# GpSimd copies released by the VectorE operation ahead of the planned SBUF copy instead of by the copy itself

## Chip, cores and metric

One core of one Trainium2 chip. The metric is the time of one execution in microseconds of device time, the median of several runs. The profiler's span of the same execution is about 1.8 us shorter than that time; trace times below count from the span's start.

## The reference, cut to what matters

```python
def reference(A_x, A_wqkv, A_wo, B_x, B_w_gate, B_w_up, B_w_down, gate_w):
    # x: 1 x 2048 x 512, bf16; 32 heads of 16; gated MLP of width 1376
    g = sigmoid((A_x * gate_w).sum(-1, keepdims=True))
    a = attention(A_x, A_wqkv, A_wo)      # softmax(q k^T / 4) v, then wo
    b = ((A_x @ B_w_gate) * (A_x @ B_w_up)) @ B_w_down
    return g * a + (1 - g) * b
```

The bulk is 32 heads x 2048 x 2048 exponentials of attention scores.

## The kernel before: the parts that the change touches

The exponentials are shared out. ScalarE computes most of them (line 1689: exp from PSUM into bf16 tiles in SBUF, 1024 or 1536 columns at a time). For the rest, VectorE evicts a score tile from PSUM (reads it there and writes it to SBUF) as an integer approximation of its exponential (line 1076), and the three other quarters of that key block are had from the same tile by adding a constant to the int16 pattern: an SBUF-to-SBUF copy, run either by VectorE (line 1154) or by GpSimd (line 1157):

```python
if eng == "dve":      # VectorE
    fn = lambda v: v.tensor_single_scalar(cell_ap(c, I16), cell_ap(src, I16), 32.0 * k, ALU.add)
else:                 # GpSimd
    fn = lambda g: g.tensor_scalar(cell_ap(c, I16), cell_ap(src, I16), 32.0 * k, 1.0, ALU.add, ALU.mult)
```

The kernel is laid out by a planner in Python, which keeps a clock per engine with assumed durations and appends each operation with its dependencies; semaphore waits are made from these. VectorE's copies and GpSimd's use the same pair of SBUF ports, called the port below, and the one that comes second waits (1.27 us for 0.41 in the lines at 73 us that the prediction shows). The planner keeps VectorE's copies and GpSimd's operations apart in time, and makes GpSimd wait on the chip for the last VectorE copy planned before it:

```python
def gen_step(eng):
    t = clock[eng]
    if eng == "pool" and t < lock["dve"]:          # GpSimd not during a VectorE copy
        clock[eng] = lock["dve"]
        return True
    ...                                            # best = a ready operation of the queue
    if eng in ("dve", "pool") and (best is None or best.prio > CPR):
        if eng == "pool" or lock["pool"] <= t:     # VectorE copy not during GpSimd
            c = try_copy(eng, t)
            if c is not None:
                if eng == "dve":
                    lock["op"] = c                 # the copy to wait for
                elif lock["op"] is not None:
                    c.deps.append(lock["op"])      # GpSimd waits for it
                run_task(c, t)
                lock[eng] = clock[eng]
                return True
    ...
    if eng == "pool" and lock["op"] is not None:
        best.deps.append(lock["op"])               # so do GpSimd's other operations
    run_task(best, t)
```

VectorE never waits for GpSimd for the port's sake; if GpSimd runs late, the two meet on the chip.

The softmax here doesn't subtract the row's maximum and nothing guards it: scores larger than these inputs give would overflow.

## Time and profile before

| | before |
|---|---|
| time, median (range, runs) | 715.96 us (715.78 to 716.11, 3) |
| span of the profiled run | 714.4 us, granted clock 0.998 |
| busy: TensorE, VectorE, ScalarE, GpSimd | 96%, 91%, 98%, 59% |
| longest chain | ScalarE 63%, GpSimd 0% |

The page's own lines are shown in the prediction.

### The profile page before, as it was taken

What the parts mean: (1) busy time and instruction counts of PE and PEld (TensorE: products, weight loads), DVE (VectorE), ACT (ScalarE), POOL (GpSimd) and SP (SyncE); (2) the same over time, 40 slices, a digit from 0 to 9 for tenths busy, and PEclk for the clock granted to TensorE, in tenths of its full rate; (3) what the DMA queues carried; (4) which work ended last, traced back from release to release, by engine and by line L of the source; (5) the groups of instructions that cost most, each with busy time, mean ns of one, the idle gap of its engine ahead of it and who ended that gap; (6) DMA issues with size and microseconds to landing.
All of it is one profiled execution on the core that took longest, in us unless ns stands there. A gap on an engine that the chain in (4) does not pass through costs nothing.

```text
span 714.4 us, 21301 instructions
## 1 busy us (share of the span) xinstructions
PE 687.7 (96%) x9115; PEld 188.3 (26%) x9115; DVE 649.1 (91%) x1229; ACT 699.9 (98%) x689; POOL 424.7 (59%) x463
## 2 busy tenths in 40 slices
PE   8999899999999999999999999999999999999997
PEld 3323232222222222222222222222222222222222
DVE  5999989998998889899988998999889988998887
ACT  6999999999999999999999999999999999999995
POOL 4547676555556575566477556555557676555572
PEclk9999999999999999999999999999999999999999
DMA  6800001000200001000000010000000001000001
GB/s 140 257 12 8 21 17 18 21 17 16 86 21 18 17 11 35 28 17 17 20 3 28 17 43 26 18 11 12 21 18 17 15 29 31 17 21 18 3 20 46
DMA packets 33054, 21.65 MB, mean 30 GB/s; under 512 B 20380, under 2 KB 27964, under 8 KB 32960
## 3 DMA queue, kind: packets, MB, share of 16 engines
q1 hardware_dynamic: 31632, 19.64, 9.4%
q8 instruction: 71, 1.16, 0.7%
q10 hardware_dynamic: 1328, 0.66, 0.4%
q14 instruction: 23, 0.19, 0.1%
HBM read 15.12 MB, written 2.36 MB: 24 GB/s over the span
## 4 chain that ended last, share of the span: by engine, by line
ACT 63%; PE 22%; DVE 8%; issue 3%; SPq 2%; DMA 1%; POOL 0%; DVEq 0%; POOLq 0%
ACT PT L1689 57%; PE psS L488 8%; PE psO L1219 7%; PE psX L557 5%; ACT wv L1689 4%; SPq L322 2%; ACT wd L1689 2%; DVE PT L1076 2%; DVE PT L1154 1%; DVE wd L1076 1%; PE psS L557 1%; PE psX L667 1%; DVE QM L632 1%; PE psX L488 1%; DMA xT<-in_A_x_dram 1%
## 5 line engine op out<-in xcount | busy, mean ns | idle before, releaser
L1689 ACT ACTIVATE PT<-psS 128x1024 bf16<-128x1024 f32 (+1 forms) x577 | 624.8, 1413 | 1.2 <-PE psS L488 0.8
L1157 POOL TENSOR_SCALAR PT<-PT 128x1024 int16<-128x1024 int16 x220 | 228.2, 1047 | 161.5 <-DVE PT L1154 81.2
L488 PE MATMUL psS<-QM,KE 32*128 32x512 bf16 x1968 | 255.4, 376 | 10.7 <-ACT PT L1689 5.4
L1076 DVE TENSOR_SCALAR PT<-psS 128x512 int16<-128x512 f32 x328 | 221.6, 684 | 22.5 <-PE psS L488 18.5
L1219 PE MATMUL psO<-PT,VS 128*18 128x512 bf16 x1709 | 227.9, 381 | 0.7 <-DVE oraw L1248 0.6
L1219 PE MATMUL psO<-PT,VD 128*18 128x512 bf16 x1231 | 192.3, 381 | 0.6 <-DVE wd L1154 0.6
L1017 PEld LDWEIGHTS <-KE 32*128 32x128 bf16 x2048 | 63.1, 91 | 278.1 <-issue 144.9
L1154 DVE TENSOR_SCALAR PT<-PT 128x1024 int16<-128x1024 int16 (+1 forms) x232 | 105.3, 482 | 2.2 <-PE psO L1219 1.0
L1157 POOL TENSOR_SCALAR PT<-wv 128x1024 int16<-128x1024 int16 x57 | 59.1, 1047 | 39.7 <-DVE PT L1154 15.0
L1219 PEld LDWEIGHTS psO<-PT,VS 128*18 128x18 bf16 x1709 | 52.1, 88 | 61.0 <-issue 43.6
L1689 ACT ACTIVATE wv<-psS 128x1024 bf16<-128x1024 f32 (+1 forms) x47 | 59.7, 1300 | 0.0
L557 PE MATMUL psX<-wd,hT 128*32 128x512 bf16 (+1 forms) x704 | 59.0, 386 | 0.0
L1076 DVE TENSOR_SCALAR wv<-psS 128x512 int16<-128x512 f32 x76 | 51.8, 686 | 6.2 <-PE psS L488 5.8
L1219 PEld LDWEIGHTS psO<-PT,VD 128*18 128x18 bf16 x1231 | 45.4, 88 | 36.9 <-issue 23.4
L557 PE MATMUL psX<-xT,wu 128*32 128x512 bf16 x688 | 53.2, 383 | 1.2 <-DVE wv L1076 0.8
L557 PE MATMUL psX<-xT,wg 128*32 128x512 bf16 x688 | 52.5, 383 | 1.5 <-DVE PT L1076 1.2
L1219 PE MATMUL psO<-wv,VS 128*18 128x512 bf16 x182 | 49.9, 381 | 0.2 <-DVE oraw L1248 0.2
L1076 DVE TENSOR_SCALAR PT<-psX 128x512 int16<-128x512 f32 x58 | 39.7, 684 | 6.8 <-PE psS L488 6.6
L1689 ACT ACTIVATE wd<-psS 128x1024 bf16<-128x1024 f32 (+1 forms) x35 | 40.3, 1222 | 0.4 <-PE psS L488 0.4
L1219 PE MATMUL psO<-wv,VD 128*18 128x512 bf16 x167 | 38.2, 381 | 0.0
L1157 POOL TENSOR_SCALAR wv<-PT 128x1024 int16<-128x1024 int16 x24 | 25.1, 1047 | 18.7 <-PE psO L1219 3.6
L488 PE MATMUL psX<-QM,KE 32*128 32x512 bf16 x80 | 30.1, 377 | 4.0 <-DVE VS L687 0.9
(127 smaller groups left out, 703.3 us busy)
## 6 DMA issues: line engine op xcount, KB each, us to landing
rb<-rscr SPq DMA_DIRECT2D x31, 256.0 KB
out_dram<-ost SPq DMA_DIRECT2D x12, 128.0 KB, 1.7
wu<-in_B_w_up_dram SPq DMA_DIRECT2D x1, 1376.0 KB, 9.2
wg<-in_B_w_gate_dram SPq DMA_DIRECT2D x1, 1376.0 KB, 12.1
wd<-in_B_w_down_dram SPq DMA_DIRECT2D x1, 1280.0 KB, 6.0
OT<-OX SPq DMA_DIRECT2D x60, 16.0 KB, 1.8
wo<-in_A_wo_dram SPq DMA_DIRECT2D x1, 512.0 KB, 12.6
out_dram<-wk SPq DMA_DIRECT2D x4, 128.0 KB, 1.7
```

Of the source, the lines that this page charges most:

```text
L322: return now(eng, deps, lambda e: e.dma_start(dst, src, **kw), occ, lat=lat, stream=stream, dma=True)
L488: return e.add_instruction(mybir.InstMatmult(name=nc.get_next_instruction_name(), engine=mybir.EngineType.PE, ins=[e.lower_ap(rhs), e.lowe ...
L557: return e.matmul(out_ap[32 * q : 32 * q + w, :], lhs[:, 32 * q : 32 * q + w], rhs, start=s0, stop=s1, tile_position=(0, 32 * q), skip_gro ...
L632: lambda v, p=p: v.tensor_scalar(QM[:, p, b, :], qtmp[:], mask[:, p : p + 1], None, ALU.mult),
L667: r = e.matmul(bk.ap[32 * q : 32 * q + 32, t2 * 256 : (t2 + 1) * 256], xT[:, kt, t * 128 + 32 * q : t * 128 + 32 * q + 32], wv[:, kt, bp * ...
L1017: r = e.ldweights(w, tile_position=pos)
L1076: lambda v: v.tensor_scalar(cell_ap(pr["cell"][i : i + 1], mybir.dt.int16), bk.ap, CB, 0.0, ALU.add, ALU.max),
L1154: fn = lambda v: v.tensor_single_scalar(cell_ap(c, I16), cell_ap(src, I16), 32.0 * k, ALU.add)
L1157: fn = lambda g: g.tensor_scalar(cell_ap(c, I16), cell_ap(src, I16), 32.0 * k, 1.0, ALU.add, ALU.mult)
L1219: r = e.matmul(psO[32 * j : 32 * j + VW, :], pv_stationary(m, kt, j, k), cell_ap((cell,)), start=s0, stop=s1, tile_position=(0, 32 * j), s ...
L1689: lambda a: a.activation(cell_ap(c), src, ACT.Exp, scale=LN2 / 128.0),
```

## The change

Intent: GpSimd should not lose the time of a semaphore's way after each VectorE copy. It is let go when the operation ahead of the copy ends; the copy, which follows at once, is expected to be on the shared port first and to hold GpSimd back by itself. Below, such a release of GpSimd around one VectorE copy is called a handover. The diff in its core:

```diff
-        lock = {"dve": 0.0, "pool": 0.0, "op": None}
+        lock = {"dve": 0.0, "pool": 0.0, "op": None, "prev": None}
...
                         if eng == "dve":
-                            lock["op"] = c
+                            lock["op"] = lock["prev"]
+                            lock["prev"] = c
...
             run_task(best, t)
+            if eng == "dve":
+                lock["prev"] = best
```

## The prediction

> **What bounds the kernel now.** I read the page from the top: busy shares, then the chain of waits that ended last, then the groups, and only then the waits of single engines. The busy table and the chain:
>
> ```profile
> PE 687.7 (96%) x9115; PEld 188.3 (26%) x9115; DVE 649.1 (91%) x1229; ACT 699.9 (98%) x689; POOL 424.7 (59%) x463
> ACT 63%; PE 22%; DVE 8%; issue 3%; SPq 2%; DMA 1%; POOL 0%; DVEq 0%; POOLq 0%
> ```
>
> ScalarE (ACT) is busy for 699.9 of 714.4 us and carries 63% of the chain; GpSimd (POOL) carries 0%. Three engines are over 90%, so I asked who waits. The view of waits, ScalarE alone:
>
> ```profile
> ACT L369 <- issue: 2.4, 1, 2.4
> ACT oraw L1903 <- PE psS L557: 2.1, 1, 2.1
> ACT xT L1807 <- PE psS L1797: 1.5, 1, 1.5
> ACT KE L587 <- PE psS L557: 1.4, 1, 1.4
> ACT PT L1689 <- PE psS L488: 0.8, 3, 0.4
> ACT wd L1689 <- PE psS L488: 0.4, 1, 0.4
> ACT hT L1689 <- PE psS L488: 0.2, 1, 0.2
> ```
>
> The columns are microseconds in total, times, longest. The first four lines are start and tail. In between, from about 9 to 705 us, ScalarE waits 0.8+0.4+0.2 = 1.4 us for scores, and nothing else. Its exponentials complete at a fixed pace (in the records one ends 917 ns after the one before if it covers 1024 columns, 1343 ns if 1536), so this stretch is a solid train of 674 instructions that no other engine can shorten by more than those 1.4 us.
>
> Now the operations that the change touches: GpSimd's copies (line 1157) and VectorE's copies (line 1154) of the same kind, SBUF to SBUF, int16.
>
> ```profile
> L1157 POOL TENSOR_SCALAR PT<-PT 128x1024 int16<-128x1024 int16 x220 | 228.2, 1047 | 161.5 <-DVE PT L1154 81.2
> L1154 DVE TENSOR_SCALAR PT<-PT 128x1024 int16<-128x1024 int16 (+1 forms) x232 | 105.3, 482 | 2.2 <-PE psO L1219 1.0
> ```
>
> GpSimd stands idle for 161.5 us ahead of its largest group, half of it put down to VectorE copies. That looks like a prize, but the view of line 1157 also says who waits for these copies:
>
> ```profile
> who waited for it (us, times):
>   PEld psO L1219: 1.4, 5
> ```
>
> 1.4 us in five waits, all by TensorE, and none by ScalarE. So earlier GpSimd results are worth almost nothing, and the real question is whether earlier GpSimd starts harm VectorE, which shares a port with it.
>
> **What the Trainium skill says.** "SBUF — State Buffer", section "Who interferes with whom": VectorE and GpSimd share one SBUF port pair; a VectorE instruction in a two-port mode and a GpSimd instruction exclude each other, the first to start holds the pair for its whole length, the other blocks. "VectorE: DVE Perf Modes", section "Mode 4×_2P": a one-input 16-bit SBUF-to-SBUF operation takes both ports and does 4 elements per cycle. The trace agrees with both. Unblocked copies of 1024 and of 2048 columns take about 412 and 682 ns, 270 ns for 1024 more columns, which is 4 per cycle at the 0.96 GHz that the skill states. And blocking is visible. VectorE and GpSimd around 73 us, from the timelines of the two engines:
>
> ```profile
> 72.87 0.42 DVE L1154 TENSOR_SCALAR PT<-wd 128x1024 int16<-128x1024 int16 x1
> 73.20 1.27 DVE L1154 TENSOR_SCALAR PT<-PT 128x1024 int16<-128x1024 int16 x1
> 72.89 1.30 POOL L1157 TENSOR_SCALAR wd<-PT 128x1024 int16<-128x1024 int16 x1
> ```
>
> GpSimd's copy starts 23 ns after VectorE's first one, is held (1.30 us for 1.05), takes the port when that one lets go, and the second VectorE copy, queued right behind, then waits for GpSimd: 1.27 us for 0.41. By the records to the nanosecond, GpSimd ends 901 ns after the first copy's end, and the second copy ends 279 ns after GpSimd's. This is the planned situation of the changed kernel in miniature. (The skill's "Perfetto Trace Analysis", section "GPSIMD Engine Instruction", calls GpSimd spans unreliable; here the starts and ends are consistent to a few ns, and I use ends.)
>
> **The change, part by part.** The kernel is scheduled by a Python planner, and the planned order is untouched: comparing the two built programs, each engine has the same instructions in the same order, only waits move. In 280 GpSimd instructions the VectorE instruction waited for is now exactly one place earlier: instead of the last planned copy, the one ahead of it (183 times itself a copy, 77 times a PSUM eviction of line 1076, 20 others). Real data dependencies are kept by their own waits.
>
> - *Which were held by that wait.* Laying the program's waits over the trace, 184 of the 280 start within 160 ns of the end of the copy waited for: 63 at about 83 ns, 121 at about 155 ns (those that have a second wait ahead of it). The others come later, mostly queued behind another GpSimd instruction.
> - *When they start now.* VectorE's instructions overlap a little: a ready copy is recorded as starting about 79 ns before the end of its predecessor, and ends 334 ns after that. Released by the predecessor, GpSimd starts 83 or 155 ns after that end, so about 162 or 234 ns after the copy has started. The copy is first and has the port, as in the pair above. GpSimd blocks and takes the port when the copy lets go, ending 901 ns after the copy's end. Today it ends 83+1047 = 1130 or 155+1047 = 1202 ns after. Gain: 229 or 301 ns each, an estimate that rests on one instance. In each of the 184 cases the GpSimd instruction before had ended at least 0.36 us earlier, so there is room.
> - *What that looks like.* Recorded spans grow, because blocked time counts as busy: 334-83+901 = 1152 ns (63 times) and 334-155+901 = 1080 ns (121 times) for 1047. POOL busy rises by 63×0.105 + 121×0.033 = 10.6 us, to about 435.
> - *Where VectorE gains.* 62 of its 419 copies are blocked today, 19.8 us over their 412 or 682 ns in sum. Behind 36 of them stands a GpSimd instruction that now ends 0.23 to 0.30 us earlier (directly, or pushed back to back). Taking that off each, down to zero, removes 8.0 us.
> - *Where VectorE loses.* In 18 of the 184 the copy itself was late, 8 to 106 ns after its predecessor's end. In three GpSimd would come 10 to 23 ns ahead of it and may win: about 0.85 us each. And in three more (at 81, 137 and 485 us) a second two-port instruction (line 632) follows the copy at once; today it slips in before GpSimd, now GpSimd should take the port first, again 0.85 us. Together at most 6 × 0.85 = 5.1 us.
>
> Sum on VectorE: between -8.0 and -2.9 us of 649.1, so some 641 to 646. Of this nothing lies on the path: today's 62 blocked copies, up to 0.87 us each, cost ScalarE at most its 1.4 us of waits. Sum on the kernel: between -1.4 us, if every wait for scores were owed to VectorE, and a few tenths lost by a new one. I take -0.2.
>
> **Rivals.**
>
> 1. *GpSimd is paced by VectorE, and frees buffers and results earlier.* For it: 161.5 us of idle before one group. Against: the plan leaves GpSimd idle at 59% busy, its consumers waited 1.4 us, and ScalarE is full. Even granted in full it gives 1.4 us, time 714.5.
> 2. *GpSimd takes the port ahead of VectorE's copies.* If a queued GpSimd instruction had priority, or if it started as soon as the predecessor's result is visible while the copy is not yet under way, up to 184 copies would be blocked by some 0.85 us: 156 us on an engine with 65 us of slack, and VectorE would become the bound, at about 800 us. Against: the copy is recorded as 160 to 230 ns ahead, GpSimd was held by a copy only 23 ns ahead of it at 72.89 us, and where a VectorE instruction and a second GpSimd instruction both waited (62.16 us) VectorE got in between them. A milder form, 20 to 30 copies lost, would be 20 us of VectorE time, still within its slack, and cost perhaps 1 to 3 us by single late evictions.
> 3. *The copies were being blocked today by late GpSimd instructions, and VectorE is the hidden pacer.* Then 8 us off VectorE would show. Against: TensorE is 96% busy and ScalarE follows without gaps; VectorE's gain becomes idle time.
>
> **Range and chances.** The three runs before lie within 0.33 us. The best case is 714.5, the plain case 715.8, the milder form of rival 2 reaches 718. I predict 715.7, with 714.6 to 717.2 to hold it 8 times in 10. Over 2% faster (under 701.6) would need ScalarE's train to be shorter, which nothing here does: 0.005. Over 2% slower (over 730.3) needs rival 2 nearly in full: 0.02. Within 2%: 0.975.
>
> **What would show it.** ScalarE busy unchanged at 700 us and its waits in the middle between 0.5 and 3 us; mean durations of line 1157 up from 1047 to about 1074 over all (52 and 121 of the 350 in the two clusters at 1152 and 1080); the idle time before it put less to line 1154; line 1154 in sum no longer than before, with no crowd of copies at 1.27 us; PE and DMA as before. Wrong would be: many copies at about 1.27 us, VectorE busy above 655, GpSimd spans still at 1047 starting before the copies, or new ScalarE waits for scores behind blocked evictions.

## More of the kernel before

One more view matters later: busy time of each engine in two stretches of the kernel before (start:end and length in us, then busy us of TensorE, its weight loads, VectorE, ScalarE and GpSimd, then granted clock, DMA share and GB/s).

```profile
60.00:150.00 90.00, 83.81 (x1240) 26.03 (x1236) 86.27 (x167) 89.33 (x84) 59.24 (x83) 1.00 0.07 16
150.00:700.00 550.00, 536.42 (x6914) 139.57 (x6906) 502.69 (x938) 549.28 (x534) 330.78 (x315) 1.00 0.07 22
```

VectorE is 86.27/90 = 96% busy in the first stretch and 502.69/550 = 91% in the second; ScalarE is idle for 0.67 us in the first 90 us and for 0.72 us in the other 550.

## The result

| | before | after |
|---|---|---|
| time, median (range, runs) | 716.04 us (715.78 to 716.12, 4) | 714.74 us (714.55 to 714.88, 4) |
| the same, repeated in the first batch of experiments | 716.19 us (11 runs) | 714.52 us (5 runs) |
| span of the profiled run | 714.4 us | 713.1 us |

The ratio is 0.9982 (95% interval 0.9965 to 1.0), in the repeat 0.9978 (0.9966 to 0.999). Ratios are the mean time of one kernel's fast runs over that of the other's fast runs of the same rounds, so not quite the ratio of the medians. The gain is 1.3 us, 0.2%, in the repeat 1.7 us. The time lies within the predicted range, 0.14 us above its low end of 714.6 us; the repeat lies 0.08 us below that end.

The page of the changed kernel, its busy line and the two groups:

```profile
PE 688.0 (96%) x9115; PEld 188.2 (26%) x9115; DVE 643.2 (90%) x1229; ACT 699.1 (98%) x689; POOL 439.2 (62%) x463
L1157 POOL TENSOR_SCALAR PT<-PT 128x1024 int16<-128x1024 int16 x220 | 237.0, 1086 | 146.1 <-DVE PT L1154 38.9
L1154 DVE TENSOR_SCALAR PT<-PT 128x1024 int16<-128x1024 int16 (+1 forms) x232 | 101.4, 466 | 2.1 <-PE psO L1219 0.8
```

VectorE lost 5.9 us of busy time, GpSimd gained 14.5 us of it (time spent waiting at the port counts as busy), and the idle time put down to line 1154 halved. The planned handover, from the timelines of VectorE and GpSimd:

```profile
308.17 0.76 DVE L1154 TENSOR_SCALAR PT<-PT 128x1024 int16<-128x1024 int16 x2
308.67 1.15 POOL L1157 TENSOR_SCALAR PT<-PT 128x1024 int16<-128x1024 int16 x1 [0.94 <-DVE PT L1154]
```

Two VectorE copies run from 308.17 to 308.93. GpSimd is released by the first of them, starts during the second, is held (1.15 us for 1.04 to 1.05) and ends at 309.82, 0.9 us after the second copy's end. In the kernel before, the same pair stood at 309.32 to 310.07 and GpSimd ran from 310.15 to 311.20, so it ended 1.13 us after the pair:

```profile
309.32 0.75 DVE L1154 TENSOR_SCALAR PT<-PT 128x1024 int16<-128x1024 int16 x2
310.15 1.05 POOL L1157 TENSOR_SCALAR PT<-PT 128x1024 int16<-128x1024 int16 x1 [0.97 <-DVE PT L1154]
```

Over the 184 handovers, GpSimd's end comes 901 ns (median; middle half 900 to 902) after the copy's end.

What ScalarE waits for, in the changed kernel (its lines between start and tail):

```profile
ACT PT L1689 <- PE psS L488: 0.6, 2, 0.4
ACT hT L1689 <- PE psS L488: 0.2, 1, 0.2
```

That is 0.8 us where it was 1.4: 0.6 of the 1.3 us. The rest is hidden from this view. A queued exponential of 1024 columns is recorded with 1362 ns, beginning under its predecessor; one that was released late is recorded with about 1024 ns. The delay shortens the overlap before it opens a gap. So I measured lateness by ends: for each exponential, its end less the end before it, less the pace (917 ns for 1024 columns, 1343 for 1536), summed over a stretch.

| lateness of ScalarE, us | 9 to 60 us | 60 to 150 us | 150 to 705 us |
|---|---|---|---|
| before | 0.36 | 1.70 | 0.95 |
| after | 0.14 | 0.39 | 0.83 |

Of the 1.65 us gained between 9 and 705 us, 1.31 lie between 60 and 150 us. (The start-up before 9 us differs from run to run by some 0.3 us either way; in the profiled run of the changed kernel it was 0.3 us longer.) The largest single piece, 0.49 us, is the wait at 83.85 us. ScalarE's timeline before:

```profile
81.09 2.37 ACT L1689 ACTIVATE wd<-psS 128x1024 bf16<-128x1024 f32 x2
83.85 1.02 ACT L1689 ACTIVATE wd<-psS 128x1024 bf16<-128x1024 f32 x1 [0.39 <-PE psS L488]
```

and after, the same three instructions without a gap:

```profile
80.62 3.62 ACT L1689 ACTIVATE wd<-psS 128x1024 bf16<-128x1024 f32 x3
```

Its history starts at the collision around 73 us that the prediction shows. The same instructions in the changed kernel, VectorE's two and GpSimd's one:

```profile
72.95 0.69 DVE L1154 TENSOR_SCALAR PT<-wd 128x1024 int16<-128x1024 int16 x1
73.56 0.41 DVE L1154 TENSOR_SCALAR PT<-PT 128x1024 int16<-128x1024 int16 x1
72.31 1.04 POOL L1157 TENSOR_SCALAR wd<-PT 128x1024 int16<-128x1024 int16 x1
```

GpSimd comes 0.58 us earlier (it is the end of a back-to-back train of 13 that starts at 65.87 instead of 66.53 us), so the collision costs VectorE 0.28 us instead of 0.85, and VectorE, which has hardly a gap from there to 85 us, delivers everything after it half a microsecond earlier. In the trace before, the way from the blocked copy to the exponential at 83.85 us can be followed: VectorE has no recorded idle time between 71.02 and 88 us, its eviction of 82.71 us ends at 83.38 us, TensorE computes the scores from 83.44 us, and ScalarE waits for these.

The busy view of the early stretch, after the change (86.27 us of VectorE and 89.33 of ScalarE before):

```profile
60.00:150.00 90.00, 85.59 (x1258) 26.15 (x1250) 85.15 (x170) 89.95 (x86) 61.12 (x84) 1.00 0.07 16
```

Theory T after this look: the gain is VectorE's blocked port time, and only where VectorE has no idle time to take it, which is the early stretch. Rival E: GpSimd's results and freed buffers come earlier. Rival S: the gain is spread over all moved waits.

### The profile page after: what moved, and what is told of

The parts are those of the page before. It is cut to its first block, busy times and chain, and to the rows that moved or that the text cites. A ratio compares the mean times of both kernels' runs of the same rounds, so it can differ in the third digit from the quotient of the medians.

```text
span 713.1 us, 21304 instructions
## 1 busy us (share of the span) xinstructions
PE 688.0 (96%) x9115; PEld 188.2 (26%) x9115; DVE 643.2 (90%) x1229; ACT 699.1 (98%) x689; POOL 439.2 (62%) x463
## 5 line engine op out<-in xcount | busy, mean ns | idle before, releaser
L1157 POOL TENSOR_SCALAR PT<-PT 128x1024 int16<-128x1024 int16 x220 | 237.0, 1086 | 146.1 <-DVE PT L1154 38.9
L1154 DVE TENSOR_SCALAR PT<-PT 128x1024 int16<-128x1024 int16 (+1 forms) x232 | 101.4, 466 | 2.1 <-PE psO L1219 0.8
L1157 POOL TENSOR_SCALAR PT<-wv 128x1024 int16<-128x1024 int16 x57 | 61.0, 1078 | 40.9 <-DVE wv L1076 16.5
L1689 ACT ACTIVATE wd<-psS 128x1024 bf16<-128x1024 f32 (+1 forms) x35 | 42.0, 1289 | 0.0
L830 DVE TENSOR_TENSOR hT<-psX,usb 128x512 bf16<-128x512 f32 (+1 forms) x44 | 30.0, 682 | 4.4 <-PE psX L557 4.3
```

The costliest lines, as they stand in the source:

```text
L830: lambda v: v.tensor_tensor(hT[0:w, f, :], bk.ap[0:w, :], usb[0:w, n % 2, :], ALU.mult),
L1689: lambda a: a.activation(cell_ap(c), src, ACT.Exp, scale=LN2 / 128.0),
```

## The experiments

Twelve runs, in three batches; each batch has its own runs of the kernel before (medians 716.19, 716.32 and 716.35 us). "Blocked" is the time of VectorE's copies over their unblocked 412 or 682 ns, summed over those at least 25 ns over: 19.8 us in 62 copies before, 12.1 us in 43 after.

### Repeat, and the change in one part of the program

The repeat is the changed kernel itself.

> The changed kernel once more, so that the others have it on the same chip. Theory (T): the gain of 1.3 us is real, ratio to the kernel before 0.9975 to 0.9987, about 714.7 us. Rival (N, chip or run to run noise): ratio 0.999 to 1.001.

Measured: 714.52 us, ratio 0.9978 (0.9966 to 0.999), blocked 12.4 us. The gain is not noise.

Early and late part:

```diff
-                            lock["op"] = lock["prev"]
+                            lock["op"] = lock["prev"] if t < 150.0 else c     # late: t >= 150.0
```

> The earlier release only for GpSimd operations planned before 150 us (74 waits moved, 38 of them held by the copy in the trace of before); the rest as before. Theory (T): ScalarE's train was pulled in at 77 to 142 us of the trace, where VectorE runs without a gap, so this part alone brings nearly the whole gain: 714.7 to 715.0 us, VectorE busy down by 2 to 3 us only. Rival (S, the gain is spread with the waits): 74 of 280 waits give a quarter of it, 715.7 us.

> The earlier release only for GpSimd operations planned from 150 us on (206 waits moved, 146 of them held by the copy). Theory (T): little comes of it, 715.7 to 716.1 us, although VectorE loses more of its blocked time here than in the early part. Rival (S): three quarters of the gain, 715.0 us.

Measured: early 714.61 us (ratio 0.998, interval 0.9968 to 0.9992), late 716.23 us (1.0007, 0.9995 to 1.0019). Busy time from 60 to 150 us, early and then late:

```profile
60.00:150.00 90.00, 85.63 (x1255) 26.13 (x1250) 85.22 (x170) 89.94 (x86) 61.25 (x84) 1.00 0.06 16
```

```profile
60.00:150.00 90.00, 83.82 (x1240) 26.01 (x1236) 86.26 (x168) 89.34 (x85) 59.12 (x82) 1.00 0.07 16
```

The early part alone takes ScalarE's idle time from 0.67 to 0.06 us; the late part leaves it at 0.66. Both save VectorE the same: 646.2 us busy in each, 2.9 less than before. Rival S falls: 74 of the 280 moved waits bring the whole gain, 206 bring nothing. Both times came about 0.1 us outside the ranges I had written, on the favourable side for T.

### Are the lost races what limits it?

The prediction's three doubtful cases were lost, as the clearest shows, VectorE and GpSimd in the changed kernel:

```profile
226.04 1.30 DVE L1154 TENSOR_SCALAR PT<-PT 128x1024 int16<-128x1024 int16 x1
226.02 1.04 POOL L1157 TENSOR_SCALAR PT<-PT 128x1024 int16<-128x1024 int16 x1 [1.17 <-DVE PT L1076]
```

GpSimd is 22 ns ahead, and the copy takes 1.30 us instead of 0.43. To take these out, GpSimd waits for the copy itself where the planner has the copy start late:

```diff
-                            lock["op"] = lock["prev"]
+                            p_ = lock["prev"]
+                            lock["op"] = p_ if p_ is not None and t <= p_.start + p_.occ + 0.05 else c
```

> The earlier release, but where the planner starts the copy later than its predecessor ends (38 waits, among them the three lost races at 226, 234 and 649 us) GpSimd waits for the copy itself, as before. Theory (T): the three copies of 1.30 us go back to 0.42 us, VectorE busy is 1 to 4 us below that of the changed kernel, and ScalarE gets back the 84 ns that it lost at 240 us: 714.5 to 714.8 us, 0 to 0.2 below the changed kernel. Rival (R: the races are what held the change back): 714.0 us or less.

Measured: 714.71 us; no copy near 1.3 us is left, VectorE busy 642.1 us, 1.1 below the changed kernel. The time can't be told from the changed kernel's (714.52 us in the same batch; ranges overlap). The races are real and cost nothing that shows. No version here beats the changed kernel.

### How close is the edge?

Two places ahead (`prev2` is kept as `prev` is, one operation further back), and no wait for copies at all, one look each (a single run, its state unknown; a loss of 50 to 60 us needs no more):

```diff
-                            lock["op"] = lock["prev"]
-                            lock["prev"] = c
+                            lock["op"] = lock["prev2"]
+                            lock["prev2"], lock["prev"] = lock["prev"], c
```

```diff
-                        elif lock["op"] is not None:
-                            c.deps.append(lock["op"])
...
-            if eng == "pool" and lock["op"] is not None:
-                best.deps.append(lock["op"])
```

> GpSimd released by the VectorE operation two places ahead of the planned copy. Theory (T, the one-place release works because the copy is already on the port when GpSimd is let go): GpSimd now takes the port ahead of the copy in most of the 184 cases, over 100 copies of about 1.27 us, VectorE busy over 720 us and the kernel 735 to 790 us. Rival (H, the hardware sorts the two out whatever the wait, and the wait is idle): 714 to 718 us.

> GpSimd does not wait for planned copies at all, for its data and buffers alone. Theory (T): as with two places ahead, VectorE's copies are blocked in crowds, over 80 us in sum, 725 to 790 us. Rival (H): 714 to 718 us.

Measured: 776.70 and 767.17 us. The page's busy line with two places ahead, then the main wait of ScalarE there:

```profile
PE 690.0 (89%) x9115; PEld 188.9 (24%) x9115; DVE 728.8 (94%) x1229; ACT 713.4 (92%) x689; POOL 447.8 (58%) x463
```

```profile
ACT PT L1689 <- PE psS L488: 36.4, 82, 1.7
```

VectorE's copies are blocked for 116.1 us in sum (106 of them by more than 0.7 us), without any wait for 100.8 us. VectorE becomes the bound and ScalarE waits for scores in crowds. One place is right by about 160 to 240 ns, the head start of the copy; one more place costs 60 us. Rival H falls, and the port is shown to matter as T needs.

### Results late, or port held long

To tell T from E, I delayed the announcement of each GpSimd copy by a one-column memset that waits for it (slow_signal), and in another kernel left the announcement alone but let GpSimd write 160 columns of a spare tile after each copy (hold_port):

```diff
             task.op = P.op(task.eng, task.fn, ops, task.stream, 16 if task.dma else 1)
+            if task.pad:                           # GpSimd copies; pad is 1 column in slow_signal, 160 in hold_port
+                padst[0] = P.op("pool", lambda g: g.memset(pad[:, :], 0.0), [padst[0], task.op])   # hold_port: [padst[0]]
+                task.op = padst[0]                 # slow_signal only
```

> The changed kernel, but the result of every GpSimd copy is announced only by a one-column memset on GpSimd that waits for the copy, so some 0.15 to 0.25 us later, about as late as before the change; the port is given back as early as in the changed kernel. Theory (T, the gain comes from the port being free for VectorE earlier): 714.6 to 715.1 us, VectorE's blocked time near the changed kernel's 12 us. Rival (E, the gain comes from GpSimd's results and buffers being there earlier): back to 715.8 to 716.3 us.

> The changed kernel, results announced as early as there, but after every GpSimd copy GpSimd writes 160 columns of a spare tile, which keeps the port some 0.2 us longer. Theory (T): VectorE's copies are blocked again, some 18 to 24 us in sum, and the gain is lost: 715.5 to 716.5 us. Rival (E): it stays at 714.7 us.

Measured: slow_signal 716.26 us, hold_port 719.93 us. The memsets in the two kernels' groups:

```profile
L306 POOL MEMSET pad<- 128x1 bf16 x350 | 49.5, 141 | 20.8
```

```profile
L306 POOL MEMSET pad<- 128x160 bf16 x350 | 82.2, 235 | 0.0
```

Holding the port longer brings the blocked time to 42.3 us, twice what I had expected (each memset also pushes GpSimd's next instruction back), the time 3.4 us above the range that I had written, and ScalarE's lateness to 2.83 us from 60 to 150 us and 3.26 us later. The recorded waits of the other engines that ended with a GpSimd instruction are as in the changed kernel (0.45 us from 60 to 150 us and 4.4 later, for 0.50 and 4.1), so late results do not account for it: the port time counts, once it is large enough everywhere. The other run, slow_signal, decides nothing. The gain was gone, as E said, but its condition failed: the blocked time was 25.8 us instead of some 12, above the kernel before, because the extra instruction also delays GpSimd. T explains the 716.26 us as well as E does.

### VectorE's time alone

So I left GpSimd's program alone and cost VectorE time directly, at three places early or late (`padst` holds the last memset and the count of VectorE copies):

```diff
+                            if padst[1] in (37, 51, 57):       # vec_late: (187, 239, 331); number of the VectorE copy
+                                for _ in range(3):
+                                    padst[0] = P.op("dve", lambda v: v.memset(pad[:, :], 1.0), [padst[0]])
+                            padst[1] += 1
                             lock["op"] = lock["prev"]
```

> The changed kernel with GpSimd untouched, but VectorE runs three small memsets of a spare tile, by an estimate 0.6 to 0.8 us in sum, ahead of each of the three copies that were blocked longest before the change (73.2, 93.0, 100.0 us). Theory (T2: VectorE's time is what counts, and only in the stretch from about 70 to 112 us where it runs without gaps): 715.4 to 716.2 us, although all GpSimd results are as early as in the changed kernel or nearly so. Rival (E): 714.6 to 714.9 us.

> The same memsets ahead of three copies that were blocked before by 0.5 us each at 322, 406 and 566 us. Theory (T2: there VectorE has idle time that takes the delay): 714.5 to 714.9 us. Rival (V: VectorE's time counts everywhere): as with the early ones, 715.4 us or more.

Measured: vec_early 716.81 us, vec_late 715.04 us, with the kernel before at 716.35 in the same batch. The changed kernel was not run in this batch; 1.3 to 1.7 us below the kernel before, as in the two comparisons above, it would be at about 714.7 to 715.05. VectorE's memsets in vec_late:

```profile
321.27 0.78 DVE L1732 MEMSET pad<- 128x160 bf16 x3
321.96 0.69 DVE L1156 TENSOR_SCALAR PT<-PT 128x1024 int16<-128x1024 int16 x2
```

Each dose is 0.69 us to the next start, 2.1 us in the three. Early they cost 1.8 to 2.1 us. Late they cost at most some 0.35 us: vec_late came 0.14 us above the range that I had written for it, but its trace shows none of this as lateness of ScalarE (0.83 us after 150 us, as in the changed kernel). Busy from 60 to 150 us, vec_early and then vec_late, and ScalarE's new wait behind the dose at 93.40 us in vec_early:

```profile
60.00:150.00 90.00, 83.92 (x1237) 25.73 (x1228) 84.92 (x176) 88.86 (x84) 60.73 (x83) 1.00 0.06 16
```

```profile
60.00:150.00 90.00, 85.61 (x1254) 26.21 (x1250) 85.19 (x170) 89.94 (x86) 61.25 (x83) 1.00 0.07 16
```

```profile
96.91 3.83 ACT L1691 ACTIVATE PT<-psS 128x1536 bf16<-128x1536 f32 x3 [0.67 <-PE psS L490]
```

Lateness of ScalarE from 60 to 150 us is 2.01 us with the early doses and 0.41 with the late ones (0.39 in the changed kernel). vec_early came 0.6 us above the range that I had written; the doses at 73 and 93 us reached ScalarE in full (0.71 and 0.90 us; behind the second a copy was blocked again), that at 100 us not at all. VectorE's time in the early stretch is enough to move the kernel by as much as the change does. (The doses delay GpSimd too, wherever it waits for VectorE; what that is worth is looked at under the rivals below.)

### Four waits

```diff
-                            lock["op"] = lock["prev"]
+                            lock["op"] = lock["prev"] if 60.0 <= t < 68.0 else c      # no_spot: not 60.0 <= t < 68.0
```

> The kernel before with only 4 of its 280 waits moved (GpSimd copies at 61.2, 62.2, 66.5 and 67.5 us of the trace of before; two of them were held directly). Theory (T2: GpSimd ran late in a back-to-back train from 66.5 us on, its last instruction at 72.89 us cost a VectorE copy 0.85 us, and that delay reached ScalarE at 77 to 85 us): the copy at 73.2 us falls from 1.27 to about 0.42 to 0.7 us and the kernel gains 0.6 to 0.75 us: 715.3 us. Rival (E, many GpSimd results that come earlier): no gain, 716.0 us or more.

> The changed kernel with just those 4 waits put back. Theory (T2): the block at 73 us returns and ScalarE loses the 0.72 us of 77 to 85 us again: 715.2 to 715.5 us. Rival (E): 714.6 us as the changed kernel.

Measured: no_spot 715.40 us (715.12 to 715.42), some 0.35 to 0.7 above the changed kernel's place in this batch, and in the range that T2 gave (715.2 to 715.5). In the traces its lateness from 60 to 150 us is 0.87 us against 0.39 in the changed kernel, so the four waits are worth 0.48 us, all of it between 78 and 85 us. Its copy at 73 us takes 1.17 us.

spot gave 715.47, 715.51, 715.95, 717.42 and 717.92 us, median 715.95. By these times the run decides nothing: the ratio to the kernel before is 0.9995 (0.9981 to 1.0008), and 715.95 us lies between T2's 715.3 and E's 716.0, nearer to E's. Its profile fell on the slowest run. Busy from 106 to 109 and from 109 to 114 us:

```profile
106.00:109.00 3.00, 2.15 (x34) 0.60 (x26) 3.00 (x6) 3.00 (x4) 1.98 (x3) 1.00 0.02 5
109.00:114.00 5.00, 4.57 (x62) 1.61 (x66) 3.66 (x8) 3.79 (x4) 2.85 (x5) 0.66 0.02 2
```

The clock record of the trace stands at 0.50 from 109.62 to 113.03 us and at 1.00 around it (so 0.66 over these 5 us); why it fell is not shown. Meanwhile matmuls take about 0.6 us for 0.38, and ScalarE loses 1.32 us. Without that piece, its lateness from 60 to 150 us is 2.64 - 1.32 = 1.32 us, 0.38 below the kernel before, all of it between 77 and 85 us; the copy behind GpSimd takes 0.89 us instead of 1.27. So in the two traces T2 had the place and the sign right, and the size was half to two thirds of the 0.72 us expected: in the changed kernel, part of GpSimd's 0.58 us lead at 73 us was gained earlier. Single runs of 717 to 718 us also occurred in other kernels and in the kernel before; of these only this one has a trace. (The traces of two_ahead and nolock have three such falls to 0.50 each.)

## Why the prediction was right, and where it missed

The handover works as predicted; what it is worth to the kernel was mis-sized, and the range held by 0.14 us only, with its low end set by a cap that was read too small. That much of it was luck.

- **Bound (right).** ScalarE's train is the bound: busy 699.1 us after, 699.9 before, with the same pace.
- **The handover (right).** A gain of 229 or 301 ns per handover was read off one pair of instructions at 72.89 us: GpSimd's end 901 ns after the copy's. In the 184 cases the median is 901 ns, and GpSimd's end moved against the copy by a median of 292 ns, with a tenth at 303 or more and three quarters at 229 or more.
- **GpSimd's spans (right in kind, small in size).** Predicted 1152 and 1080 ns, total 435 us busy; measured clusters at 1140 to 1160 (34) and 1070 to 1090 (74), and 439.2 us. I had left out copies longer than 412 ns (blocked themselves, or 2048 columns), behind which GpSimd waits longer: 29 spans are over 1200 ns.
- **VectorE's gain (right).** Expected 8.0 us off the blocked copies and at most 5.1 back; measured 19.8 to 12.1 us, busy 649.1 to 643.2.
- **The three races (right).** All three, 9 to 22 ns ahead, were lost, about 0.87 us each. The nearest that the copy won had it 49 ns ahead.
- **Line 632 (wrong).** "a second two-port instruction (line 632) follows the copy at once; today it slips in before GpSimd, now GpSimd should take the port first, again 0.85 us". GpSimd does go first, but line 632 comes in pairs. Before, the first of a pair slipped in and the second was blocked (1168, 1168 and 1161 ns); now the first is blocked (1125, 1132 and 1130 ns) and the second is free. The term is about zero.
- **What of it is on the path (mis-sized).** "I take -0.2" was -1.3. The step that failed is "Of this nothing lies on the path": most of it does not, as the late part shows, but blocked copies between 70 and 112 us did. Two errors lie behind it. The cap of 1.4 us was read from gaps between ScalarE's records, while its lateness by ends was 3.0 us (0.36 + 1.70 + 0.95), of which 1.65 us were gained, more than that cap. And I judged VectorE by its 65 us of slack over the whole span instead of by stretch: from 60 to 150 us it was 96% busy, with 6.4 of the 19.8 us of blocked time before 150 us (2.4 after).
- **Rivals.** Rival 1, GpSimd's earlier results and buffers (E in the experiments), has little for it: waits of TensorE for line 1157 rose from 1.4 to 2.7 us while the time fell. The one run that was to exclude it, slow_signal, was spoilt, but the trace of the kernel before bounds it: between 60 and 150 us, where 1.31 us were gained, a single wait of any other engine ended with a GpSimd instruction, 0.2 us of a weight load (the last line of this section). And vec_early and vec_late show VectorE's time moving the kernel by this much early and hardly late. Rival 3, VectorE as hidden pacer, which the prediction argued away with "VectorE's gain becomes idle time", holds for 60 to 150 us. Rival 2 was one place away, and at "about 800 us" fairly sized: 776.70.

```profile
who waited for it (us, times):
  PEld psO L1219: 2.7, 10
  POOL PT L1157: 0.6, 1
```

(The view of line 1157 in the changed kernel.) And the only wait for GpSimd in the kernel before, from its waits with --window 60:150:

```profile
PEld psO L1219 <- POOL hT L1157: 0.2, 1, 0.2
```

## What to carry to other kernels

Where two engines share a port and one of them is known to be first, releasing the other one operation early lets the hardware do the handover, here 0.23 to 0.30 us sooner each; the margin is the head start of the first, and past it the loss is many times the gain. Judge the slack of an engine next to the bound stretch by stretch, and measure the bound engine's lateness by the ends of its instructions, because overlapping records hide short delays. Three quarters of the moved waits did nothing for the time.

## What the Trainium skill lacked or had wrong

- "SBUF — State Buffer", section "Who interferes with whom", has the pair held for the whole instruction. By the records it is let go earlier: a GpSimd copy held by a VectorE copy ends 901 ns after it, for 1043 to 1047 ns of its own, so it began in effect about 145 ns before that copy's recorded end, if it then took its usual time. The other way round, a held copy of 1024 columns ends 279 ns after GpSimd's recorded end, for 412 ns of its own. Whether the port is free before the instruction ends, or only the record runs on past that, these runs do not show.
- The same page says that who starts first wins, but not how near: GpSimd recorded 9 to 22 ns ahead of the copy won all three times; a copy 23 ns ahead of GpSimd at 72.89 us (kernel before) won.
- No page that I read gives the time from the end of a VectorE instruction to the start of a GpSimd one that waits for it: 83 ns with one wait, about 155 ns with a second wait ahead of it.
- "Perfetto Trace Analysis", section "GPSIMD Engine Instruction", calls GpSimd spans unreliable; here ends were steady to a few ns over 184 handovers, and the lengthened spans showed the blocking.
- "Perfetto Trace Analysis", section "DVE / Act Engine Instruction", does not say that a recorded span depends on whether the instruction was queued: the same ScalarE exponential of 1024 columns is recorded with 1362 ns when queued and about 1024 ns when released late, at a pace of 917 ns from end to end.
